# Fourier layer and soft mixture of experts on one core: slot logits of two steps made in one block on TensorE, with the order of the batch chains and the split of copies set anew

## The chip, the core and the metric

The kernel runs on 1 core of one Trainium2 chip, as one launch. The metric is the time of one execution in microseconds (us) as the device gives it; less is better. The program works in fp32; many matmuls are made as three fp32r products of a rounded high part and the rest ("h" and "l" in the names), which gives them nearly fp32's precision.

## What is computed

```python
X = np.fft.rfft(x, axis=1)                      # x: 8 x 2496 x 256
Yr = Xr @ w_r - Xi @ w_i + b_r                  # w: 256 x 256
Yi = Xr @ w_i + Xi @ w_r + b_i
Yr = np.sign(Yr) * np.maximum(np.abs(Yr) - 0.01, 0.0)    # Yi the same
y = np.fft.irfft(Yr + 1j * Yi, n=2496, axis=1)
x = y.reshape(19968, 256)
logits = x @ phi                                # 32 slots, 4 for each of 8 experts
d = np.exp(logits - logits.max(0)); d /= d.sum(0) + 1e-9     # over all tokens
slot_input = d.T @ x
slot_out = np.maximum(slot_input @ w1[e], 0) @ w2[e]         # per expert, F = 1024
c = np.exp(logits - logits.max(1)); c /= c.sum(1) + 1e-9     # over the slots
out = c @ slot_out
```

## The kernel before

**The idea.** 2496 = 39 x 64, so each transform is made in two stages of matmuls, a 39-point one and a 64-point one. The kernel never makes y: phi, the slot sums and the inverse transform are linear, so the slot logits are taken in the frequency domain and transformed back with 32 columns in place of 256, and the slot inputs are summed there as well.

**The work of a batch** (8 batches b) is cut into 5 steps of 4 frequencies (`KG`), so there are 40 steps s, with grp = s mod 5. On TensorE (PE) a step makes:

- `pa` (`a_unit`, L368): the 39-point stage of a later batch, 11 units of three 512-column matmuls for each batch. Its input x is split into `xh` (a rounding copy, line with `E_("ah")`) and `xl` (a subtraction). ScalarE (ACT) copies `pa` to `ast`, which goes through DRAM to `ap`.
- `px` (`f2`, L437): the 64-point stage, two halves; ACT and VectorE (DVE) make `xth`, `xtl`, `xsm`, `xsh` and GpSimd (POOL) `xsl` from it.
- `pk` (`lin_k`, L509) and `py` (`lin_y`, L520): the complex 256 x 256 product, in three real products. DVE adds them to `ut`; the soft threshold is ut - clip(ut): a clip (`TENSOR_SCALAR rt<-ut`, by the table "th") and a subtraction on POOL (`TENSOR_TENSOR rt<-ut,rt`, "tl").
- `pq` (`tp_p`, L550): the slot logits of the step, phi (128 x 32 a half) against `rt`. Only 32 of the array's 128 columns are needed, so four matmuls, one for each frequency, stand side by side in four column strips: L569-576. ACT copies the 128 x 128 result to `lg`, PE transposes it into the same bank, DVE multiplies it with a sign into `p_sb`.
- `pt` (`tp_t`, L586): eight transposes of `rt`; the copies `T` out of PSUM go by the table "te".

**The chain of a batch** (`c_stages`, L671) begins when its `p_sb` is complete and runs beside the steps of the next batches: `pg`, a trip through DRAM, `pL` (logits in the time domain), the maximum over tokens (`pm`, `pb`), exp, the way back (`pe`, DRAM, `pd`) to `dd`, and then the slot sums `pr` (`slots_acc`, L810; five groups of 8 matmuls, 32 columns wide, four side by side like `pq`), which multiply `dd` with the `T` tiles of the batch. `c_comb` (L604) makes the softmax over the slots beside it. For batch 7, `last_chain` (L1064) does the same without DRAM; behind it stand the experts' two layers (`hps`, `po`) and the output loop (`pq<-rhs,ct`), whose 156 matmuls feed the stores of the result.

**What sets the order.** Every piece of work is a generator that yields a due time and then issues its instructions; a heap (`step_to`, `run_until`, L854) runs the earliest first, and one unit of this time is a quarter of a step. Each engine then works strictly in that written order. The due times are the numbers in `PLAN` (L138): "tp" are those of `tp_p`, "tt" those of `tp_t`, "pr", "pm", "pb", "pe", "pd" those of a chain, "late" the ones for batches 4 to 6, "T_" those of the end. A letter string such as "AV" deals the instructions of a kind out in turn: A is ACT, V is DVE, P is POOL. The last 24 clips and subtractions have a table of their own ("lth", "ltl"). All DMA issues on SP keep the written order too. Tiles of one tag share buffers in rotation: `pt`, `pf`, `pl` have two PSUM banks each, `ps` and `pr` one; "T" has 20 tiles, "rt" 4.

Of the kernel before, what the change touches and what calls it, by code (L numbers as in the profile page):

```python
# [220 lines left out]
def fourier_soft_moe_kernel(ctx: ExitStack, tc: tile.TileContext, t: dict, out: bass.AP):  # L221
# [60 lines left out]
    def mm(**kw):  # L282
        tc.keep_in_program_order(nc.tensor.matmul(**kw))  # L283
# [299 lines left out]
    def tr(out, in_, identity):
        tc.keep_in_program_order(nc.tensor.transpose(out=out, in_=in_, identity=identity))  # L584
# [797 lines left out]
```

## Time and profile before

| | us |
|---|---|
| three timed runs | 532.81, 536.44, 533.71 (median 533.71) |
| the profiled execution | 534.27, with a span of 532.4 from the first instruction to the last |
| start, up to the first steps | 0 to 45 |
| the steps of batches 0 to 7 beside the chains | 45 to 427 |
| end of the last steps and the chain of batch 7 | 427 to 456.6 |
| the experts (`hps`, `po`) | 456.6 to 474 |
| output loop and last stores | 474 to 532.4 |

In the profile, a row of the timeline gives the start of an instruction in us from the span's start, its duration, the engine and what it writes and reads; "x16" are 16 neighbouring instructions of one kind. PE is TensorE's matmul, PEld its weight load. An fp32 matmul stands as two instructions. A matmul's duration is longer than the distance to the next start, since matmuls overlap: of dense rows the distance from start to start is the cost. "Idle before" is the time in which the engine did nothing ahead of the instruction, with who released it.

### The profile page before, as it was taken

The numbers are of one execution on the slowest core, as the hardware profiler recorded it, in microseconds if no ns is written. First come the engines' busy times: TensorE is split into PE (matmuls) and PEld (weight loads), VectorE is DVE, ScalarE is ACT, GpSimd is POOL, SyncE is SP. The second block draws the span as 40 slices with busy tenths as digits, with TensorE's granted clock in tenths as the row PEclk, the third lists the DMA queues.
The fourth block names the chain that finished last, engine by engine and source line by source line (L and its number), as shares of the span: only waits on it lengthen the run. The fifth ranks groups of instructions, "written<-read, shape, count | busy, mean of one in ns | idle before, by whom it ended". The sixth has DMA issues, their size and how long they took to land.

```text
span 532.4 us, 12136 instructions
## 1 busy us (share of the span) xinstructions
PE 509.8 (96%) x4512; PEld 437.7 (82%) x4512; DVE 406.1 (76%) x801; ACT 304.5 (57%) x683; POOL 316.8 (59%) x300
## 2 busy tenths in 40 slices
PE   8889999999999999999999999999999999899991
PEld 4478999998999899998989899988989877368880
DVE  3277988689978988998789878987878686337671
ACT  4346565667665766566657656765564336037770
POOL 0049687667976787578757876897457521414210
PEclk9999999999999999999999999999999999899997
DMA  8999575757686667566766666796967489329998
GB/s 299 270 321 321 162 219 159 216 175 151 221 228 175 143 216 211 186 150 217 202 189 147 225 169 204 162 324 170 267 153 187 124 335 372 116 107 388 403 405 326
DMA packets 84799, 119.99 MB, mean 225 GB/s; under 512 B 38380, under 2 KB 59372, under 8 KB 84740
## 3 DMA queue, kind: packets, MB, share of 16 engines
q1 hardware_dynamic: 83796, 117.08, 71.7%
q10 hardware_dynamic: 944, 2.13, 1.4%
q8 instruction: 36, 0.59, 0.5%
q14 instruction: 23, 0.19, 0.1%
HBM read 69.19 MB, written 50.00 MB: 224 GB/s over the span
## 4 chain that ended last, share of the span: by engine, by line
PE 86%; DMA 4%; DVE 4%; ACT 2%; SPq 1%; issue 1%; POOL 0%; DVEq 0%; ACTq 0%
PE py L283 20%; PE px L283 12%; PE pa L283 11%; PE pq L283 10%; PE pk L283 10%; PE pt L584 6%; PE pr L283 3%; PE hps L283 2%; PE pL L283 2%; PE pc L584 2%; PE pd L283 2%; PE pe L283 2%; PE pg L283 1%; PE po L283 1%; DMA ap<-ad 1%; DMA xr<-in_x 1%
## 5 line engine op out<-in xcount | busy, mean ns | idle before, releaser
L217 POOL TENSOR_TENSOR rt<-ut,rt 128x512 f32<-128x512 f32 x79 | 112.6, 1425 | 16.4 <-DVE rt L217 15.8
L217 POOL TENSOR_TENSOR xl<-xr,xh 117x512 fp32r<-117x512 f32 x73 | 99.2, 1360 | 16.5 <-PE py L283 8.8
L217 POOL TENSOR_TENSOR xsl<-xsm,xsh 128x256 fp32r<-128x256 f32 x77 | 59.3, 770 | 77.4 <-DVE xsh L217 54.1
L283 PE MATMUL px<-smov,ap 128*128 128x128 f32 x640 | 85.1, 276 | 1.9 <-ACT ast L217 1.0
L283 PEld LDWEIGHTS px<-smov,ap 128*128 128x128 f32 x640 | 79.9, 191 | 7.4 <-ACT ast L217 2.0
L217 ACT COPY ast<-pa 128x512 f32<-128x512 f32 x85 | 50.0, 589 | 57.2 <-PE pa L283 55.4
L217 DVE SCALAR_TENSOR_TENSOR ut<-py,pk,k 128x256 f32<-128x256 f32 x160 | 69.6, 476 | 13.0 <-PE py L283 11.5
L217 ACT CAST xth<-px 128x512 fp32r<-128x512 f32 x80 | 46.8, 587 | 47.2 <-PE py L283 30.9
L217 DVE TENSOR_TENSOR xtl<-px,xth 128x512 fp32r<-128x512 f32 x80 | 54.6, 684 | 20.0 <-ACT xsm L217 19.6
L217 DVE TENSOR_SCALAR rt<-ut 128x512 f32<-128x512 f32 x69 | 57.3, 831 | 0.5
L283 PE MATMUL py<-xth,nwsh 128*128 128x256 f32 x160 | 54.1, 338 | 0.1
L217 ACT COPY T<-pt 128x512 f32<-128x512 f32 x80 | 47.3, 602 | 1.8 <-PE pt L584 1.8
L283 PE MATMUL pk<-xsh,w_rh 128*128 128x256 f32 x160 | 48.0, 300 | 0.0
L584 PE MATMUL pt<-pk,rt 128*128 128x128 f32 x320 | 47.4, 274 | 0.6 <-DVE p_sb L217 0.3
L283 PE MATMUL pk<-xsl,w_rh 128*128 128x256 f32 x160 | 45.2, 283 | 0.0
L283 PE MATMUL py<-xth,wdh 128*128 128x256 f32 x160 | 45.2, 282 | 0.0
L283 PE MATMUL pk<-xsh,w_rl 128*128 128x256 f32 x160 | 45.1, 282 | 0.0
L283 PE MATMUL py<-xth,wdl 128*128 128x256 f32 x160 | 45.1, 282 | 0.0
L283 PE MATMUL py<-xtl,nwsh 128*128 128x256 f32 x160 | 45.1, 282 | 0.0
L283 PE MATMUL py<-xth,nwsl 128*128 128x256 f32 x160 | 45.1, 282 | 0.0
L283 PE MATMUL py<-xtl,wdh 128*128 128x256 f32 x160 | 45.1, 282 | 0.0
L283 PE MATMUL pq<-rhs,ct 128*128 128x512 f32 x156 | 41.9, 406 | 0.2 <-DVE rhs L217 0.2
(206 smaller groups left out, 1265.7 us busy)
## 6 DMA issues: line engine op xcount, KB each, us to landing
ap<-adr SPq DMA_DIRECT2D x76, 256.0 KB
out<-ost SPq DMA_DIRECT2D x37, 512.0 KB
xr<-in_x SPq DMA_DIRECT2D x35, 512.0 KB
adr<-ast SPq DMA_DIRECT2D x20, 768.0 KB
w<-in_moe_w SPq DMA_DIRECT2D x20, 512.0 KB
w<-in_moe_w SPq DMA_DIRECT2D x18, 256.0 KB
adr<-ast SPq DMA_DIRECT2D x8, 512.0 KB
x<-in_x SPq DMA_DIRECT2D x11, 256.0 KB
```

The lines of the kernel that those rows point to most:

```text
L217: return lambda *a, **k: self.tc.keep_in_program_order(f(*a, **k))
L283: tc.keep_in_program_order(nc.tensor.matmul(**kw))
L584: tc.keep_in_program_order(nc.tensor.transpose(out=out, in_=in_, identity=identity))
```

## The change

**Two steps in one block.** `tp_p` leaves out the odd group of a pair (groups 1 and 3, in all batches but the last); at the next step a new `tp_pair` makes the logits of both steps in one run of matmuls into one PSUM bank (256 columns), with one copy to `lg` (256 wide), two transposes and one multiplication by the sign (256 wide). Group 0 stays alone. `rt` gets a fifth buffer.

**Slot sums with them.** The due times "pr" put the groups of slot sums two by two beside such a block: groups 0 and 1 ahead of the logits of group 0, groups 2 and 3 behind the pair of groups 1+2, group 4 ahead of the pair 3+4.

**Order and split.** `pm`, `pb`, the second `pe` and the second `pd` of a chain come at other due times; `pt` of the first half stands earlier. All `xh` copies of batches 2 to 7 go to ACT ("AV" to "A"), every third clip up to step 27 to POOL ("V" to "VVP"), every fourth `T` copy to DVE ("A" to "AAAV").

**The end.** The last three steps of batch 6's softmax over slots (`cs6`, its reciprocal and the multiplication) come behind the last slot sum; the four zeroed tiles `z1` to `z4` are made together with `z0`, and so take their "T" buffers ahead of the last four weight loads; two dummy matmuls stand on PE between the last slot sum and the next layer.

```diff
-    "ah": 'AV',
+    "ah": 'A',
-    "th": 'V',
+    "th": 'VVP',
-    "pm": 8.5,
-    "pb": 9.8,
-    "pe": [11.35, 12.35],
+    "pm": 9.045,
+    "pb": 10.163,
+    "pe": [11.35, 12.044],
-    "pd": [17.12, 17.75],
-    "pr": [20.49, 24.49, 28.49, 32.489999999999995, 36.489999999999995],
+    "pd": [17.12, 18.008],
+    "pr": [20.48, 20.459, 28.647, 28.49, 36.49],
...
-    "late": {'6': {'cms': [13.1, 13.2, 18, 21.85, 21.9, 22.5],
+    "late": {'6': {'cms': [13.1, 13.2, 18, 22.65, 22.66, 22.67],
-    "T_": {'du': [], 'z': 1.72,
+    "T_": {'du': [[2.55, 2]], 'z': 1.686,
-    "te": 'A',
-    "tp": [0.5, 1.0, 1.9, 1.8],
-    "tt": [2, 2.505],
+    "te": 'AAAV',
+    "tp": [0.5, 1.0, 1.784, 1.8],
+    "tt": [1.616, 2.505],
+    "tpp": [0.5, 0.731, 1.719, 1.8],
...
@@ tp_p
-        yield n + d[0]
+        pair = b < B - 1 and grp > 0
+        if pair and grp % 2:
+            return
+        yield n + (PLAN["tpp"] if pair else d)[0]
...
+        if pair:
+            yield from tp_pair(s, n, PLAN["tpp"])
+            return
...
+    def tp_pair(s, n, d):
+        b, grp = steps[s]
+        pq = psum("pt", f"pq{b}_{grp}")
+        for i in range(2):
+            rv = [tts[(s - 1 + i, e)].rearrange("p j c q -> p j (c q)") for e in range(2)]
+            for e in range(2):
+                for j in range(KG):
+                    mm(out=pq[S * j : S * j + S, 128 * i : 128 * i + 128], lhsT=phr[:, e, :],
+                       rhs=rv[e][:, j], start=(e == 0), stop=(e == 1), skip_group_check=True)
+        yield n + d[1]
+        lg = wtile([128, 256], F32, "lg", f"lg{b}_{grp}")
+        A.copy(out=lg, in_=pq[:, 0:256])
+        yield n + d[2]
+        for i in range(2):
+            tr(pq[:, 256 + 128 * i : 384 + 128 * i], lg[:, 128 * i : 128 * i + 128], ident)
+        yield n + d[3]
+        ks = slice(grp * KG - KG, grp * KG + KG)
+        V.tensor_tensor(out=psb[b][:, ks, :], in0=pq[:, 256:512].rearrange("p (j s) -> p j s", s=S),
+                        in1=sgn[:, ks].unsqueeze(2).broadcast_to([128, 2 * KG, S]), op=ALU.mult)
```

How the order moves on PE, in the steps 17 and 18 (`py3_2`, `py3_3`: batch 3, groups 2 and 3), where the logits of groups 1 and 2 of batch 3 and the slot sums of batch 1 are made. Before, PE has two runs of the 32-column kind there; the first is:

```order
L283 MATMUL pr1_2867<-T1_1_0_1481,dd1_2581 32x256 x2
L283 MATMUL pr1_2867<-T1_1_1_1507,dd1_2581 32x256 x2
L283 MATMUL pq3_1_3053<-rt3_1_0_2849,pk0_112 32x128 x4
L283 MATMUL pq3_1_3053<-rt3_1_1_2921,pk0_112 32x128 x4
L283 MATMUL py3_2_1_3042<-xth3_2_1_2888,nwsh_228 128x256
```

and the second, a step later:

```order
L283 MATMUL pr1_2867<-T1_2_0_1640,dd1_2581 32x256 x2
L283 MATMUL pr1_2867<-T1_2_1_1670,dd1_2581 32x256 x2
L283 MATMUL pq3_2_3216<-rt3_2_0_3031,pk0_112 32x128 x4
L283 MATMUL pq3_2_3216<-rt3_2_1_3087,pk0_112 32x128 x4
L706 MATMUL pm2_3225<-pk0_112,mx2_3197 128x117
```

Now there is one run, at the second place, with both steps' logits and two groups of slot sums; at the first place `py` goes through without a break, and `pm2` is no longer behind the run:

```order
L284 MATMUL pq3_2_3175<-rt3_1_0_2825,pk0_112 32x128 x4
L284 MATMUL pq3_2_3175<-rt3_1_1_2901,pk0_112 32x128 x4
L284 MATMUL pq3_2_3175<-rt3_2_0_3011,pk0_112 32x128 x4
L284 MATMUL pq3_2_3175<-rt3_2_1_3052,pk0_112 32x128 x4
L284 MATMUL pr1_2840<-T1_2_0_1596,dd1_2539 32x256 x2
L284 MATMUL pr1_2840<-T1_2_1_1658,dd1_2539 32x256 x2
L284 MATMUL pr1_2840<-T1_3_0_1750,dd1_2539 32x256 x2
L284 MATMUL pr1_2840<-T1_3_1_1802,dd1_2539 32x256 x2
L284 MATMUL py3_3_1_3168<-xth3_3_1_3029,nwsh_228 128x256
```

Over the whole order of PE, the runs in which only `pq`, `pr` and `pz` (a one-column sum that opens a chain's slot sums) of 32 columns stand fall from 42 to 28: 14 fewer, two in each of the batches 0 to 6.

The end on DVE, from the last two multiplications into `dd` of batch 7 to the copy into `z0`. Before, the sums `cs` of batch 6 stand between them and `zacc`:

```order
L217 TENSOR_TENSOR dd7_6814<-pd7_1_6851,pk1_113 128x320 [waits PE_49]
L217 TENSOR_REDUCE cs6_6585<-cb6_6583 128x22
L217 TENSOR_SCALAR cs6_6585<-cs6_6585 128x22 [waits DVE_49]
L217 RECIPROCAL cs6_6585<-cs6_6585 128x22 [waits DVE_49]
L217 SCALAR_TENSOR_TENSOR zacc_121<-zacc_121,fo_120,pz7_6885 128x1 [waits PE_49,Activation_49]
L217 TENSOR_SCALAR zacc_121<-zacc_121 128x1 [waits DVE_49]
L217 RECIPROCAL zacc_121<-zacc_121 128x1 [waits DVE_49]
L217 TENSOR_SCALAR dgs_123<-pk1_113,zacc_121 128x32 [waits DVE_49]
L217 SCALAR_TENSOR_TENSOR acc_122<-acc_122,fo_120,pr7_6872 128x256 [waits PE_49]
L217 COPY z0_6855<-psl1_6906 128x8x4 [waits PE_49,Pool_49]
```

Now they stand behind that copy, and with them POOL's multiplication `cb6`, which waits for them:

```order
L218 TENSOR_TENSOR dd7_6758<-pd7_1_6795,pk1_113 128x320 [waits PE_49]
L218 SCALAR_TENSOR_TENSOR zacc_121<-zacc_121,fo_120,pz7_6833 128x1 [waits PE_49,Activation_49]
L218 TENSOR_SCALAR zacc_121<-zacc_121 128x1 [waits DVE_49]
L218 RECIPROCAL zacc_121<-zacc_121 128x1 [waits DVE_49]
L218 TENSOR_SCALAR dgs_123<-pk1_113,zacc_121 128x32 [waits DVE_49]
L218 SCALAR_TENSOR_TENSOR acc_122<-acc_122,fo_120,pr7_6820 128x256 [waits PE_49]
L218 COPY z0_6798<-psl1_6857 128x8x4 [waits PE_49,Pool_49]
L218 TENSOR_REDUCE cs6_6529<-cb6_6527 128x22
L218 TENSOR_SCALAR cs6_6529<-cs6_6529 128x22 [waits DVE_49]
L218 RECIPROCAL cs6_6529<-cs6_6529 128x22 [waits DVE_49]
```

What moved is only the place of the three `cs6` instructions; `acc` and the copy into `z0`, on which the experts' first matmul waits, come three instructions earlier.

More of the change, by code (lines that the diff above doesn't have):

```diff
@@ L145 @@
     "c0": 0.05,
-    "pg": [1.35, 2.3],
+    "pg": [1.408, 2.3],
     "pL": [6.6, 7.3],
-    "pm": 8.5,
-    "pb": 9.8,
-    "pe": [11.35, 12.35],
+    "pm": 9.045,
+    "pb": 10.163,
+    "pe": [11.35, 12.044],
     "cm": 14.3,
-    "pd": [17.12, 17.75],
-    "pr": [20.49, 24.49, 28.49, 32.489999999999995, 36.489999999999995],
+    "pd": [17.12, 18.008],
+    "pr": [20.48, 20.459, 28.647, 28.49, 36.49],
     "au": [1.4, 18.85, 19.7],
@@ L158 @@
     "xlo": 1.1,
-    "sho": 0.2,
+    "sho": 0.359,
     "slo": 0.1,
@@ new lines @@
+    "late": {'6': {'cms': [13.1, 13.2, 18, 22.65, 22.66, 22.67], 'pd': [16.681, 16.6], 'pdt': ('pl', 'pl'), 'pr': [17.15, 18.3, 20.179, 19.707, 19.902], 'pL': [6.6, 7.3], 'pm': 8.51, 'pb': 9.45, 'pe': [11.747, 11.6, 12.419], 'pg': [0.875, 1.275], 'fr': {'sinv': 0, 'm2': 0, 'f1': 0, 'suni': 0}, 'pbx': 1.5, 'pet': ('pf', 'pf'), 'so': 0.2}, '5': {'pr': [33.585, 35.378, 40.05, 40.06, 40.157]}, '4': {}},
+    "T_": {'wl': [[-45, 'r', 1], [-44, 'r', 1], [-43, 'r', 1], [-31.0, 't', 1], [-30.7, 't', 1], [-29.4, 't', 2], [-27.8, 't', 2], [-27.6, 't', 2], [-24, 't', 2], [-22, 't', 2], [-20, 't', 2], [-12.5, 'R', 1], [-12.4, 'R', 1], [-11.4, 's', 1], [-11, 'a', 1], [-10.3, 'a', 1], [-9.6, 'a', 1], [-9.5, 'Ww_r', 1], [-8.7, 'Wnws', 1], [-8.6, 'Wwd', 1], [0.01, 'k', 1], [0.01, 'u', 1], [0.02, 'x', 2], [0.02, 'x', 2], [0.02, 'x', 2], [1.4, 't', 2], [1.4, 't', 2], [1.4, 't', 2], [1.4, 't', 2], [1.4, 't', 2], [1.73, 'T', 2], [1.74, 'T', 2]], 'cl': 2.0, 'cp': 46.5, 'ct': 46.6, 'du': [[2.55, 2]], 'd1': [], 'cm': [19.9, 19.91, 19.92, 25, 25.1, 25.2], 'cm7': [0.71, 1.7, 1.95, 2.7, 2.71, 2.8], 'ye': 0.2, 'te': [[5.6, 0.2], [5.5, 0.4]], 'pg': [-17, -13.5, -8.3, -3.934, -2.9], 'yt': 0.578, 'wr': -30.6, 'tp': [0, 0.6, 0.85, 0.5], 'tt': [0.4, 0.55, 0.821, 1.25, 0.994], 'z': 1.686, 'th': [0.1, 0.12], 'tl': [0.2, 0.25], 'pgt': ['ps', 'ps', 'ps', 'pf', 'pf'], 'ch': [0.263, 0.5, 0.7, 1.0, 1.514, 2.0], 'te7': 'AAAAAAAAAA', 'op': 2, 'ot': [3, 5, 7], 'gt': [-16.99, -13.49, -8.290000000000001, -3.9400000000000004, -2.89]},
@@ L197 @@
     "xl0": 1.0,
-    "pbx": 0.45,
+    "pbx": 0.543,
     "pet": ('ps', 'ps'),
@@ L234, in fourier_soft_moe_kernel @@
     a_bufs = {"xr": 3, "xh": 3, "xl": 3, "ast": 3}
-    main_bufs = {"xsm": 2, "k1": 2, "ut": 2, "rt": 4, "lg": 2}
+    main_bufs = {"xsm": 2, "k1": 2, "ut": 2, "rt": 5, "lg": 2}
     chain_bufs = {"wr": NWR, "ap": 3, "xth": 3, "xtl": 3, "xsh": 3, "xsl": 3, "T": 20, "p_sb": 2, "g_sb": 1,
@@ L570, in tp_p @@
         yield n + d[1]
-        lg = wtile([128, 128], F32, "lg", f"lg{b}_{grp}")
-        A.copy(out=lg, in_=pq[:, 0:128])
+        lg = wtile([128, 256], F32, "lg", f"lg{b}_{grp}")
+        A.copy(out=lg[:, 0:128], in_=pq[:, 0:128])
         yield n + d[2]
-        tr(pq[:, 128:256], lg, ident)
+        tr(pq[:, 128:256], lg[:, 0:128], ident)
         yield n + d[3]
@@ L579, in tp_p @@
             in1=sgn[:, ks].unsqueeze(2).broadcast_to([128, KG, S]),
+            op=ALU.mult,
+        )
+    def tp_pair(s, n, d):
[5 more added lines that the diff above has]
+                for j in range(KG):
+                    mm(
+                        out=pq[S * j : S * j + S, 128 * i : 128 * i + 128],
+                        lhsT=phr[:, e, :],
+                        rhs=rv[e][:, j],
+                        start=(e == 0),
+                        stop=(e == 1),
+                        skip_group_check=True,
+                    )
+        yield n + d[1]
+        lg = wtile([128, 256], F32, "lg", f"lg{b}_{grp}")
+        A.copy(out=lg, in_=pq[:, 0:256])
[4 more added lines that the diff above has]
+        ks = slice(grp * KG - KG, grp * KG + KG)
+        V.tensor_tensor(
+            out=psb[b][:, ks, :],
+            in0=pq[:, 256:512].rearrange("p (j s) -> p j s", s=S),
+            in1=sgn[:, ks].unsqueeze(2).broadcast_to([128, 2 * KG, S]),
             op=ALU.mult,
@@ L1020, in slot_stationary @@
     def slot_stationary():
-        pools["slz"] = wtile([128, 2, E, 32], F32, "T", "z0")
-        P.memset(pools["slz"], 0.0)
+        zs = [wtile([128, 2, E, 32], F32, "T", f"z{i}") for i in range(5)]
+        for z in zs:
+            P.memset(z, 0.0)
+        pools["slz"], pools["hz"] = zs[0], zs[1:]
     def ap_load(s):
@@ L1059, in dummy @@
     def dummy(n):
-        dps = psum("ps", f"dps{next(seq)}")
+        dps = psum("pt", f"dps{next(seq)}")
         for _ in range(n):
@@ L1200, in fourier_soft_moe_kernel @@
     P.tensor_copy(out=dmr, in_=dmask)
-    pools["hz"] = [wtile([128, 2, E, 32], F32, "T", f"z{i}") for i in range(1, 5)]
-    for z in pools["hz"]:
-        P.memset(z, 0.0)
     rhs = []
```

2 lines of the change are left out of this document (removed).

## The prediction, made before the changed kernel was run

> **What bounds the kernel now.** I read the page first: which engine is busy, and through which engine the chain runs that ended last. Then one long window over the steps, 45 to 425 us (busy us and count of PE, PEld, DVE, ACT, POOL).
>
> ```profile
> PE 509.8 (96%) x4512; PEld 437.7 (82%) x4512; DVE 406.1 (76%) x801; ACT 304.5 (57%) x683; POOL 316.8 (59%) x300
> PE 86%; DMA 4%; DVE 4%; ACT 2%; SPq 1%; issue 1%; POOL 0%; DVEq 0%; ACTq 0%
> 45.00:425.00 380.00, 377.81 (x3461) 344.66 (x3462) 324.53 (x636) 231.20 (x521) 279.46 (x254) 1.00 0.70 194
> ```
>
> Over the steps PE is busy for 377.81 of 380.00 us at a granted clock of 1.00, DVE for 85%, POOL for 74%, ACT for 61%. PE sets the pace there, so only what shortens PE's own sequence shortens the steps. But a busy PE isn't a dense PE: a matmul's duration covers its successor's start. So I looked in the timeline at distances from start to start, around one run of slot logits:
>
> ```profile
> 63.31 0.28 PE L283 MATMUL py<-xth,wdl 128*128 128x256 f32 x1
> 63.43 0.28 PE L283 MATMUL py<-xtl,wdh 128*128 128x256 f32 x1
> 63.64 0.64 PE L283 MATMUL pq<-rt,pk 128*32 128x128 f32 x16
> 64.22 0.39 PE L283 MATMUL py<-xth,nwsh 128*128 128x256 f32 x1
> 64.44 0.28 PE L283 MATMUL py<-xth,nwsl 128*128 128x256 f32 x1
> ```
>
> Dense `py` rows stand 0.12 us apart (63.31, 63.43). Around the run there is 0.21 from the last `py` to the first `pq`, and 0.22 from the first `py` behind it to the second. The weight load of that first `py` is not hidden either: see the waits below. A later run, with slot sums in front:
>
> ```profile
> 239.20 0.28 PE L283 MATMUL py<-xtl,wdh 128*128 128x256 f32 x1
> 239.41 0.64 PE L283 MATMUL pr<-T,dd 128*32 128x256 f32 x8
> 239.86 0.62 PE L283 MATMUL pq<-rt,pk 128*32 128x128 f32 x16
> 240.41 0.38 PE L283 MATMUL py<-xth,nwsh 128*128 128x256 f32 x1
> 240.64 0.28 PE L283 MATMUL py<-xth,nwsl 128*128 128x256 f32 x1
> ```
>
> It shows the same 0.21 on entry and 0.23 behind, and nothing between `pr` and `pq`: the break belongs to the change between 128 and 32 columns, not to `pq`.
>
> **Term 1, the runs.** What does a run cost beside its work? From the last full matmul ahead to the second behind, the first run takes 64.44 - 63.43 = 1.01, the second 240.64 - 239.20 = 1.44. The second has 8 `pr` more: two rounds of 256 columns, four side by side, cost 0.43. The four rounds of 128 columns of `pq` are as many columns, so 0.43 too. Then 1.01 - 0.43 - 2 x 0.12 = 0.34 is neither kind's work. Taken by `pq`'s own rounds ((0.64 - 0.28) / 3 = 0.12 each, 0.48) it is 0.29. I take 0.33. The order has 42 runs before and 28 after, with the same matmuls in them: 14 x 0.33 = **-4.6** (bounds 14 x 0.29 = -4.1 and 14 x 0.34 = -4.8). This counts in full as long as PE stays the pacemaker.
>
> **Term 2, the waits in the steps.** PE and weight-load rows of the waits (total us, times, longest):
>
> ```profile
> PEld py L283 <- issue: 5.6, 28, 0.2
> PE px L283 <- ACT ast L217: 1.0, 1, 1.0
> PE pa L283 <- POOL xl L217: 0.8, 2, 0.5
> PE pd L283 <- ACT dd L217: 0.5, 1, 0.5
> PEld pd L283 <- ACT dd L217: 2.1, 6, 0.8
> ```
>
> The first row is the exposed load behind the runs again, 0.2 each time, and no gain of its own. The last two go together: the second `pd` of a chain needs the `ps` bank that ACT empties, and came 0.63 units behind the first; now it comes 0.89 behind, with `pt`, two transposes and a `px` between them in the order. I take the matmul's own **-0.5** (bounds 0 and the 2.1 of its loads). The second `pe` comes nearer to the first (0.69 units, 1.0 before), with a `pa` and a `px` still between; I leave that in the next sum. The pair's own waits are covered: its transposes come a full `pt` behind the ACT copy, and it writes only a bank that the earlier logits shared in the same way. The odd group is later by a step, which its chain doesn't feel: a chain begins with group 4, which is not delayed. The fifth `rt` buffer covers the longer hold.
>
> **Term 3, the other engines' load.** Rows by form:
>
> ```profile
> L217 DVE TENSOR_SCALAR rt<-ut 128x512 f32<-128x512 f32 x69 | 57.3, 831 | 0.5
> L217 POOL TENSOR_SCALAR rt<-ut 128x512 f32<-128x512 f32 x11 | 7.0, 639 | 1.6 <-DVE ut L217 1.1 <-PE py L283 0.3
> L217 DVE CAST xh<-xr 117x512 fp32r<-117x512 f32 x34 | 24.9, 731 | 2.2 <-DMA xr<-in_x 2.2
> L217 ACT CAST xh<-xr 117x512 fp32r<-117x512 f32 x39 | 24.5, 632 | 2.1 <-DMA xr<-in_x 2.1
> L217 ACT COPY T<-pt 128x512 f32<-128x512 f32 x80 | 47.3, 602 | 1.8 <-PE pt L584 1.8
> L217 DVE COPY ast<-pa 128x512 f32<-128x512 f32 x3 | 2.1, 688 | 4.8 <-PE pa L283 4.8
> ```
>
> 33 `xh` casts go from DVE to ACT (-33 x 0.731 = -24.1, +33 x 0.632 = +20.9), 18 clips from DVE to POOL (-15.0, +11.5), 17 `T` copies from ACT to DVE (-10.2; +11.7 with the row of a DVE copy of that size out of PSUM). The 14 copies and 14 multiplications saved by the pairs (28 narrow ones become 14 wide ones) are off the path and left out. Sums: DVE -27.4, ACT +10.7, POOL +11.5, that is 78%, 64% and 77% of the window. None reaches PE. Busy shares hide order, though: the clip on POOL stands in the queue ahead of `xl` and `xsl`, for which `pa` and `pk` wait, and ACT's `xh` ahead of the copies that free `px` and `pa` banks. The trace doesn't have these queues. Bounds: 0, and the rows for POOL and ACT above doubled and doubled again (1.0 + 0.8, to four times as much: +5.4). I take **+0.5**, near the low end, because PE shows just three such waits in 380 us. On SP the x loads lose a wait for DVE and keep their place.
>
> **Term 4, the end of batch 7.**
>
> ```profile
> 452.55 0.87 DVE L217 TENSOR_REDUCE cs<-cb 128x22 f32<-128x704 f32 x1
> 453.53 1.05 PE L283 MATMUL pr<-T,dd 128*32 128x256 f32 x16
> 453.88 0.19 DVE L217 SCALAR_TENSOR_TENSOR zacc<-zacc,fo,pz 128x1 f32<-128x1 f32 x1
> 454.04 1.37 POOL L217 TENSOR_TENSOR cb<-cb,cs 128x704 f32<-128x704 f32 x1 [3.72 <-DVE cs L217]
> 454.49 0.96 DVE L217 TENSOR_SCALAR dgs<-pk,zacc 128x32 f32<-128x32 f32 x1
> 455.37 0.47 DVE L217 SCALAR_TENSOR_TENSOR acc<-acc,fo,pr 128x256 f32<-128x256 f32 x1
> 455.89 0.63 PE L283 MATMUL psl<-dgs,acc 128*128 128x32 f32 x4 [1.31 <-DVE acc L217]
> 456.63 3.68 PE L283 MATMUL hps<-w,z 128*32 128x512 f32 x19
> ```
>
> `pr` ends at 454.58, but `acc` starts at 455.37, behind `dgs`. That 128x32 instruction takes 0.96 and ends with POOL's `cb` (454.04 + 1.37 = 455.41); the like-sized small ones beside it take 0.2. With `cs` and `cb` moved behind, `dgs` should end near 454.7, `acc` run from there and `psl` start near 455.2: **-0.7** (bounds 0, and PE's whole idle time, -1.3). The dummies need 4 x 0.11 behind a 32-column run and end by then.
>
> The moved memsets stand on POOL before `cb`, and the last weight loads get "T" buffers freed by later transposes:
>
> ```profile
> 434.01 13.98 SPq L277 DMA_DIRECT2D w<-in_moe_w  x19
> 449.31 1.53 PE L584 MATMUL pt<-pk,rt 128*128 128x128 f32 x12
> 467.80 6.25 PE L283 MATMUL po<-w,z 128*32 128x256 f32 x112
> ```
>
> Their issue moves from 448 to about 451, with `cin0` behind them on SP; the matmuls that read them are the last of `po`, some 20 us later. Nothing; without that cover it would be 3.
>
> **Term 5, the clock.** Four windows of 3.4 us (same columns, then the granted clock):
>
> ```profile
> 454.08:457.50 3.42, 2.00 (x24) 0.83 (x19) 2.53 (x6) 0.18 (x1) 1.33 (x1) 1.00 0.24 91
> 457.50:460.91 3.41, 3.41 (x20) 0.87 (x16) 0.59 (x3) 0.00 (x0) 2.61 (x5) 0.50 0.02 5
> 13.76:17.18 3.42, 2.40 (x6) 0.87 (x6) 0.69 (x1) 0.75 (x2) 0.00 (x0) 1.00 1.02 393
> 24.00:27.42 3.42, 2.05 (x16) 1.86 (x16) 0.83 (x3) 2.14 (x6) 1.27 (x1) 1.00 1.13 241
> ```
>
> Behind the thin stretch at 454 to 457 the clock was 0.50 for 3.41 us, in the middle of `hps`: half of 3.41, 1.7 us lost. Stretches with 2.05 and 2.40 us of matmuls kept 1.00. The change closes 0.7 of the gap and lays dummies into it, so that stretch would hold about 3.0. If the clock then stays, -1.7; but I don't know in how many of the three timed runs it fell (they spread over 3.6 us). Half of it: **-0.85** (bounds 0 and -1.7).
>
> [...]
>
> **The sum.** -4.6 - 0.5 + 0.5 - 0.7 - 0.85 = -6.15 against the profiled execution's 534.27, of which 532.4 is span: 528.1. That execution lies 0.56 above the median of the runs shown, 533.71, and they are what a new measurement repeats: 533.71 - 6.15, rounded, **527.5**. The start (DMA) and the output loop have no edit in them.
>
> **Rivals.**
> 1. *The queues take part of it back* (term 3 near its bound). For it: POOL and ACT at 77% and 64% with strict order, DVE's long softmax pieces between the `T` copies. Against it: three waits in the rows. 527.5 - 0.5 + 5.4 = 532.4, so between 529.5 and 532.5. Chance 0.20.
> 2. *The runs' ends are not saved*: the break stays because a merged run waits for the later `rt`, or `py` at the old place waits for something that the break hid. For it: the odd logits now need two steps' clips. Against it: 0.34 in both runs though one has twice the work. Only terms 4 and 5 remain: 533.71 - 1.55 = 532.2. Chance 0.08.
> 3. *Slower, by ACT's queue.* Place: between `px` and its copies, where a cast of 0.632 now stands in every unit in place of every second one. If PE waits through more than 6.15 / 20.9 = 30% of the moved casts' time, the change loses; at 50% it is +10.4 - 6.15, 538.0. Against it: ACT is idle for 39% of the window. Chance 0.05.
> 4. *The memsets hold up DVE.* Five of them (2.4 us together, as long as z's five before) now lie near 445 to 448, beside DVE's maximum and exp of batch 7. In the trace POOL's `cb` stretched `dgs` by 0.75. If they stretch that chain for their whole time, 527.5 + 2.4 = 529.9. Chance 0.07.
>
> [...]
>
> **How the numbers follow.** The forecast has 0.60, its own range 525.5 to 529.5. Term 1 at -4.8, term 2 at -2.1, term 4 at -1.3 and term 5 at -1.7 together would give 524; they hardly all come. The range reaches up into rivals 1 and 4: 525.0 to 531.0. A measurement tells about 1% of this kernel from no change: 528.4 is that line. Four fifths of the forecast lie below it (0.48), and a little of rival 4 (0.02): faster 0.50; same 0.45, with rivals 1 and 2, the rest of 4 and the forecast's upper end; slower 0.05, rival 3.
>
> **What would show it.** Right: 28 such runs with 0.34 each; about -5 us between 45 and 427; `dgs` at 0.2 and `psl` 0.7 nearer to the last `pr`; the clock at 1.00 through `hps`. Wrong: new PE rows in the waits for `xl`, `ast`, `ea` or `lg` that sum to over 2 us, or a middle stretch as long as before.

## The result, and the profile after

| | before | after |
|---|---|---|
| median of 22 runs each, us | 533.44 (531.66 to 536.44) | 537.51 (534.52 to 541.62) |
| ratio to before, 95% interval | 1 | 1.0076 (1.0058 to 1.0093) |
| the profiled execution, us | 534.27, span 532.4 | 537.36, span 535.6 |

(In brackets behind a median stand the lowest and the highest run. A ratio is taken over all runs of both kernels and needn't be the quotient of the two medians; in the experiments below the two differ by up to 0.25%.)

Instead of some 6 us less, the change costs 4. The page's lines on the busy engines and the chain, and the window over the steps in the same columns as before:

```profile
PE 508.8 (95%) x4516; PEld 439.5 (82%) x4516; DVE 385.8 (72%) x753; ACT 312.8 (58%) x685; POOL 322.3 (60%) x318
PE 76%; DMA 8%; DVE 6%; ACT 3%; issue 2%; SPq 1%; POOL 0%; ACTq 0%; DVEq 0%
45.00:425.00 380.00, 372.78 (x3414) 341.71 (x3412) 300.97 (x583) 236.98 (x515) 281.24 (x268) 1.00 0.69 192
```

PE is busy for 372.8 of the 380 us, where it was 377.8, and holds 76% of the chain, where it held 86%. The load moved the way it was counted, though less of it (DVE down by 23.6 us, ACT up by 5.8, POOL by 1.8, although POOL's clips grew by 10.8 as counted: its other rows fell); no engine is full, and PE has holes. The last `pk`, at 427.1 before, starts at 432.7: the whole loss arises in the steps. PE's waits (total us, times, longest; rows that bear on nothing here are left out):

```profile
PE px L284 <- ACT ast L218: 2.6, 12, 0.3
PE pa L284 <- DMA xr<-in_x: 2.2, 1, 2.2
PE px L284 <- DVE xsm L218: 1.5, 4, 0.4
...
PE pL L284 <- ACT chpL L218: 1.3, 2, 1.1
...
PE pb L284 <- DVE dg L218: 0.7, 2, 0.5
PE pL L284 <- DVE clpL L218: 0.6, 1, 0.6
```

A single wait of 1 us for `ast` has become 12 small ones, and `pL` and `pb` wait for the chain. To see all of it, also the waits that are spread over loads, I summed the distances from one PE row's start to the next less the dense distance of its form (0.12 for 256 columns, 0.23 for 512, 0.11 for 128, and so on), from step 4's first `pk` to step 39's, by the row that came late (us, one profiled execution each; the columns on the right are experiments told below):

| late row | before | after | pairs only | letters only | chain only | xth four | cover | pL later |
|---|---|---|---|---|---|---|---|---|
| ends of the 32-column runs | 18.6 | 13.4 | 16.5 | 18.4 | 18.1 | 13.4 | 13.4 | 12.8 |
| `px` | 1.6 | 8.3 | 6.8 | 1.0 | 1.6 | 5.4 | 3.2 | 6.4 |
| `pL` | 1.8 | 4.4 | 2.9 | 2.1 | 2.2 | 4.4 | 2.4 | 1.6 |
| `pb` and `pe` | 0.7 | 2.4 | 0.3 | 0.7 | 5.7 | 3.6 | 3.6 | 3.2 |
| `pa` | 0.5 | 1.3 | 0.4 | 0.8 | 1.5 | 1.2 | 1.2 | 1.3 |
| `pt` and `pd` | 2.8 | 0.7 | 1.5 | 4.2 | 1.2 | 0.9 | 0.6 | 0.7 |
| rest | -7.8 | -6.6 | -7.5 | -7.7 | -7.7 | -6.8 | -6.9 | -6.3 |
| sum | 18.2 | 23.7 | 20.9 | 19.5 | 22.6 | 22.0 | 17.6 | 19.7 |

(The rest is below nothing because many rows stand a little denser than the figure taken for their form. In the column "cover" the 6.1 us of useless matmuls told below count as work, so its sum is without them.) The runs gave back 5.2 us, a little more than the 4.6 forecast. `px` alone took 6.7, the rows of the chain (`pL`, `pb`, `pe`) another 4.3.

**The place of a `px` wait.** Timeline of the kernel after, PE, ACT and DVE, in a step without logits (start, duration, engine; in brackets how long the engine stood idle and who ended it):

```profile
207.98 1.05 PE L284 MATMUL px<-smov,ap 128*128 128x128 f32 x8
...
209.35 0.28 PE L284 MATMUL py<-xth,wdl 128*128 128x256 f32 x1
...
209.67 0.59 ACT L218 CAST xth<-px 128x512 fp32r<-128x512 f32 x1 [0.90 <-PE py L284]
...
210.15 0.38 ACT L218 COPY xsm<-px 128x256 f32<-128x256 f32 x1
...
210.56 0.69 DVE L218 TENSOR_TENSOR xtl<-px,xth 128x512 fp32r<-128x512 f32 x1 [1.55 <-ACT xsm L218]
...
211.01 0.60 PE L621 MATMUL pt<-pk,rt 128*128 128x128 f32 x4
211.17 0.41 DVE L218 TENSOR_TENSOR xsm<-px,xsm 128x256 f32<-128x256 f32 x1
211.21 0.59 ACT L218 COPY ast<-pa 128x512 f32<-128x512 f32 x1 [0.16 <-PE pa L284]
...
211.76 0.97 PEld L284 LDWEIGHTS px<-smov,ap 128*128 128x128 f32 x8 [0.40 <-issue]
211.80 1.13 PE L284 MATMUL px<-smov,ap 128*128 128x128 f32 x8 [0.19 <-ACT ast L218]
```

`px` is done at 209.0, but ACT starts `xth` only at 209.67: there are three `xth` buffers, and the third was let go by the `py` at 209.35, the last that reads it. From there a chain frees `px`'s bank: `xth`, `xsm`, `xtl`, `xsm`, until 211.58. PE meanwhile has the last six `py`, a `pa` and four `pt`, done at about 211.45, and the next `px` could start there; it starts at 211.80. The page names ACT's `ast`, the other semaphore of that wait. But `ast` empties the other bank. `px`'s first weight load starts at 211.76, while `ast` still runs (to 211.80), and at this place of the kernel before `px` itself starts (210.77) while `ast` runs (210.43 to 211.02). The bank `px` needs is let go by DVE's `xsm`, 0.22 ahead of its start. The kernel before at the same place:

```profile
207.38 0.28 PE L283 MATMUL py<-xth,wdl 128*128 128x256 f32 x1
...
207.75 0.58 ACT L217 CAST xth<-px 128x512 fp32r<-128x512 f32 x1 [0.96 <-PE py L283]
...
208.16 0.62 PE L283 MATMUL pq<-rt,pk 128*32 128x128 f32 x16
...
209.25 0.41 DVE L217 TENSOR_TENSOR xsm<-px,xsm 128x256 f32<-128x256 f32 x1
...
210.77 1.06 PE L283 MATMUL px<-smov,ap 128*128 128x128 f32 x8
```

The same ACT wait (0.96), but a run of slot sums and logits stands between the `py` that lets `xth` go and the next `px`. The bank is free at 209.66, 1.1 us before `px` wants it.

### The profile page after: what moved, and what is told of

The parts are those of the page before. It is cut to its first block, busy times and chain, and to the rows that moved or that the text cites. A ratio compares the mean times of both kernels' runs of the same rounds, so it can differ in the third digit from the quotient of the medians.

```text
span 535.6 us, 12084 instructions
## 1 busy us (share of the span) xinstructions
PE 508.8 (95%) x4516; PEld 439.5 (82%) x4516; DVE 385.8 (72%) x753; ACT 312.8 (58%) x685; POOL 322.3 (60%) x318
## 4 chain that ended last, share of the span: by engine, by line
PE 76%; DMA 8%; DVE 6%; ACT 3%; issue 2%; SPq 1%; POOL 0%; ACTq 0%; DVEq 0%
PE py L284 18%; PE px L284 11%; PE pq L284 10%; PE pa L284 8%; PE pk L284 8%; PE pt L621 5%; PE pr L284 3%; DMA xr<-in_x 3%; DMA gd<-g_sb 2%; DMA gp<-gd 2%; PE pL L284 2%; PE pc L621 2%; PE pe L284 2%; PE pg L284 1%; DVE cb L218 1%
## 5 line engine op out<-in xcount | busy, mean ns | idle before, releaser
L218 POOL TENSOR_TENSOR rt<-ut,rt 128x512 f32<-128x512 f32 x79 | 109.6, 1388 | 21.3 <-DVE rt L218 15.5
L218 POOL TENSOR_TENSOR xl<-xr,xh 117x512 fp32r<-117x512 f32 x73 | 98.0, 1343 | 14.7 <-DVE xh L218 8.3
L284 PE MATMUL py<-xth,nwsh 128*128 128x256 f32 x160 | 52.4, 327 | 0.1
L218 ACT CAST xh<-xr 117x512 fp32r<-117x512 f32 x72 | 45.4, 633 | 2.0 <-DMA xr<-in_x 1.9
L621 PEld LDWEIGHTS pt<-pk,rt 128*128 128x128 f32 x320 | 38.0, 141 | 3.7 <-issue 0.2
```

The lines of the kernel that those rows point to most:

```text
L218: return lambda *a, **k: self.tc.keep_in_program_order(f(*a, **k))
```

## The experiments

Each time is compared with runs of the kernel before on the same chip (medians 533.66 to 534.72), in five rounds. The theories in the expectations: **Q**, ACT's and DVE's queues with the moved casts and copies (the split letters) make `px` and `pa` late. **C**, the new due times of the chain do. **F**, the loop from `px` over its copies to the next `px` is a floor that the saved runs only uncover. **W**, F made precise: the chain of 2.1 us above against PE's work in the short step. **L**, in the denser program what one place no longer waits for is waited for at the next.

**The four parts apart.** The changed kernel without one part, and the kernel before with one part. (Where values stand side by side in a diff below, they are cut out of longer lines of the kernel.) First the letters taken back:

```diff
-    "ah": 'A',  "th": 'VVP',  "te": 'AAAV',
+    "ah": 'AV', "th": 'V',    "te": 'A',
```

> The changed kernel with the three split letters put back as before (xh casts alternately on ACT and DVE, all clips on DVE, all T copies on ACT); pairs, chain order and tail stay changed. Theory Q (the engines' queues: the moved casts and copies make ACT and DVE free px's and pa's banks late): most of the some 10 us of new PE waits go, 537.5 - 5 to 8 = 529.5 to 532.5, and the waits of px for ast fall from 12 to a few. Theory C (the chain order: the second pe nearer to the first, pm, pb, pd later): little changes, 536 to 538. Theory F (the loop px, its copies, px is a floor that the saved runs only uncover): under 1.5 us of change, 536 to 538.

Measured: 539.49, ratio 1.0088 (1.0056 to 1.0121). Not faster. Q, as the cause of the loss, falls.

The chain's due times taken back:

```diff
-    "pg": [1.408, 2.3], "pm": 9.045, "pb": 10.163, "pe": [11.35, 12.044], "pd": [17.12, 18.008], "pbx": 0.543
+    "pg": [1.35, 2.3],  "pm": 8.5,   "pb": 9.8,    "pe": [11.35, 12.35],  "pd": [17.12, 17.75],  "pbx": 0.45
```

> The changed kernel with the chain's due times (pg, pm, pb, pe, pd, pbx) put back as before; pairs, split letters and tail stay changed. Theory C: the new waits go, 530 to 533. Theory Q: 536 to 538, since ACT's and DVE's queues are as long as in the changed kernel. Theory F: 536 to 538.

Measured: 536.45, 1.0028 (0.9996 to 1.0059). The time itself lies where Q and F had it; by the ratio, some 60% of the loss goes, though `pm` now cuts five merged runs in two (33 runs). The interval just touches the changed kernel's (1.0058 to 1.0093), so this run alone doesn't settle C.

The tail alone:

```diff
-'cms': [13.1, 13.2, 18, 21.85, 21.9, 22.5]   'du': []          'z': 1.72
+'cms': [13.1, 13.2, 18, 22.65, 22.66, 22.67] 'du': [[2.55, 2]] 'z': 1.686   (with slot_stationary and dummy)
```

> The kernel before with the edits of batch 7's end alone (combine work of batch 6 behind the last sum, five memsets on POOL early, dummies on PE). By the traces of the two kernels the tail gave 0.67 from the end of the steps to hps and up to 1.7 in hps where the clock did not halve. All theories: 533.4 - 0.7 to 2.4 = 531.0 to 532.7; if the clock's dip only moves with time and does not come from the thin stretch, 532.7.

Measured: 533.4, 0.9973 (0.9948 to 0.9998), that is -1.4 by the ratio (-0.1 to -2.8), within the gain of 0.7 to 2.4 that was expected; the medians are 0.8 apart.

The pairs alone (`tp_pair`, `tpp`, `pr`, five `rt`):

> The kernel before with the pairs of logits alone (14 fewer 32-column runs, slot sums due with them, the fifth rt buffer); split letters, chain order and tail as before. Theories Q and C: the pairs' saving comes through, 533.4 - 4 to 5 = 528.5 to 529.5. Theory F: what the runs save comes back as waits for px's banks, 532.5 to 534.

Measured: 536.71, 1.0049 (1.0018 to 1.0081). Slower by 2.6, although PE has nine runs fewer (in this order, too, `pm` cuts five). In the table `px` waits 5.2 more with letters and chain as they were. That is F's direction, and worse than F said.

The other way round, the changed kernel with the pairs alone undone:

> The changed kernel with the pairs alone undone (every group's logits in a run of their own, 42 runs again, four rt buffers, slot sums due as before); split letters, chain order and tail stay changed. Theory W (the pairs' short steps lose it): no more waits behind pt, and what stays is the tail's gain: 531.5 to 533.5, faster than the changed kernel although PE pays 14 runs more. Theories Q and C (letters or chain lose by themselves): 535 to 538, or 537.5 + 4.6 if the pairs' saving counts in full.

Measured: 537.84, 1.0080 (1.0056 to 1.0104). With the rest of the change in place, 14 runs more or fewer make no difference that can be seen; and the rest loses by itself. W said faster and fails on that point. Two parts of the rest are run apart next. Three more due times of the change are in none of the four parts, and no run has them alone: `tp` (1.9 to 1.784), `tt` (2 to 1.616, the earlier `pt`) and `sho` (0.2 to 0.359, the time of DVE's `xsh`). The letters alone:

> The kernel before with the three split letters of the change alone (all xh casts on ACT, every third clip on POOL, every fourth T copy on DVE). Theory Q (rival 3 of the prediction): +3 to +5, 536.5 to 538.5, by ACT's and DVE's queues ahead of px's copies. Theory C (the chain order loses): 533 to 534.5.

Measured: 535.99, 1.0020 (0.9995 to 1.0045): between the two expectations, at most a small loss. The chain's due times alone:

> The kernel before with the chain's due times of the change alone (second pe ahead of six py, second pd behind px, pm behind the run and pb behind px). Theory C: +3 to +5, 536.5 to 538.5, by waits of pe, pb and px, since ACT stands at the second pe ahead of xth. Theory Q: 533 to 534.5.

Measured: 537.5, 1.0071 (1.0043 to 1.0099): +3.8 us, the largest of the four. C holds here, but by `pb` and `pe` (table: 0.7 to 5.7), not by `px`. This place in its timeline shows why `pb` is late:

```profile
221.30 0.26 PE L706 MATMUL pm<-pk,mx 117*128 117x117 f32 x1
...
221.89 0.74 POOL L217 TENSOR_TENSOR xsl<-xsm,xsh 128x256 fp32r<-128x256 f32 x1 [2.54 <-DVE xsh L217]
221.94 0.70 DVE L217 TENSOR_TENSOR mall<-mall 128x1 f32<-128x1 f32 x1
...
222.59 1.27 POOL L217 TENSOR_TENSOR rt<-ut,rt 128x512 f32<-128x512 f32 x1
...
222.68 1.22 DVE L217 TENSOR_SCALAR dg<-pk,mall 128x32 f32<-128x32 f32 x1
...
223.95 0.39 PE L283 MATMUL pb<-dg,ones 128*117 128x32 f32 x2 [0.23 <-DVE dg L217]
```

and before:

```profile
219.33 0.32 PE L706 MATMUL pm<-pk,mx 117*128 117x117 f32 x1
...
220.00 0.16 DVE L217 TENSOR_TENSOR mall<-mall 128x1 f32<-128x1 f32 x1
220.19 0.24 DVE L217 TENSOR_SCALAR dg<-pk,mall 128x32 f32<-128x32 f32 x1
...
220.91 0.30 PE L283 MATMUL pb<-dg,ones 128*117 128x32 f32 x2
```

In the old place `pm`'s followers on DVE met an idle POOL. Put behind the run they meet POOL's `xsl` and `rt`: the 128x1 `mall` takes 0.70 and ends with `xsl` (222.64 and 222.63), the 128x32 `dg` takes 1.22 and ends with `rt` (223.90 and 223.86). It is so in most batches; the rows by form, first before, then with the chain alone (min/median/max ns):

```profile
L217 DVE TENSOR_SCALAR dg<-pk,mall x7: 241/241/242, 113.8 to 426.5; 128x32 f32<-128x32 f32 x7
```

```profile
L217 DVE TENSOR_SCALAR dg<-pk,mall x7: 242/1211/1216, 114.4 to 430.4; 128x32 f32<-128x32 f32 x7
```

From `pm` to `pb` it is now 2.65 where it was 1.58, and the chain's next steps (`exp`, `chpe`, `clpe`) can start only behind it. `pe` waits as well (three times for `clpe`, 1.5 us); how much of that comes from the stretched `dg` and how much from the second `pe`'s nearer due time, no run tells apart.

**The hole behind `pt`.** A fourth buffer for `xth`, so that ACT need not wait for `py`:

```diff
-"xth": 3,   f1a = wmp.tile([PX, QA], F32, tag="f1a", name="f1a")
+"xth": 4,   f1a = wtile([PX, QA], F32, "g7", "f1a")
```

> The changed kernel with a fourth buffer for xth (f1a moves into another tile's place to make room; no engine's order changes). Theory W: in the steps that now have no logits, px waits for a chain that begins when py lets an xth buffer go (xth 0.59, xsm 0.38, xtl 0.69, xsm 0.41: 2.1 us), while PE has only six py, a pa and four pt (1.9 us) to do; the run stood in that stretch and covered it. With a fourth buffer xth begins some 0.55 earlier, and the 12 waits of 0.38 behind pt go: -4 to -5, 532.5 to 533.5. Rival L (DVE and ACT as a whole are too loaded in the short steps, their queues set it): the start of xth isn't what matters, 536.5 to 538.

Measured: 535.77, 1.0033 (1.0012 to 1.0055), so -2.3 against the change's 1.0076, half of what W expected. The mechanism is as W has it, at the same place:

```profile
208.06 1.05 PE L284 MATMUL px<-smov,ap 128*128 128x128 f32 x8
...
209.16 0.59 ACT L218 CAST xth<-px 128x512 fp32r<-128x512 f32 x1 [0.30 <-PE px L284]
...
211.09 0.60 PE L621 MATMUL pt<-pk,rt 128*128 128x128 f32 x4
...
211.53 1.06 PE L284 MATMUL px<-smov,ap 128*128 128x128 f32 x8
```

`xth` follows its own `px`, and the next `px` stands 0.44 behind `pt`, with no gap. But `pb` and `pe` wait 1.2 more in the table: a part is taken back, which is the direction of L.

The control, the kernel before with a fourth buffer:

> Control: the kernel before with the fourth xth buffer. Theory W: a run stands in every one of those stretches there, and no wait behind pt over 0.13 is seen: no change, 532.5 to 534.5. If the buffer helps in itself, at any density of PE: -2 or more.

Measured: 534.51, 1.0005 (0.9979 to 1.0030): the buffer does nothing where the run covers the chain.

Useless work laid into the hole (an odd group's four transposes are made twice; 6.1 us more of PE):

```diff
-        for jj in range(2):
+        for jj in (0, 1, 0, 1) if h == 0 and grp in (1, 3) and b < B - 1 else (0, 1):
```

> The changed kernel with useless work on PE: the four transposes of an odd group ahead of px, in just the 14 places where the logits were taken away, are made twice (the second time the same values into the same bank): 14 x 0.44 = 6.1 us more for PE. Theory W: the stretch has a hole of 0.38 there, so about 12 x 0.38 = 4.5 of the 6.1 cost nothing: 538 to 540. If PE is dense there and the waits are made elsewhere: 537.5 + 6.1 = 543.6.

Measured: 537.26, 1.0062 (1.0036 to 1.0087). Six us of matmuls more, and no time more: even W expected some 1.5. PE does not set the pace there. The same place:

```profile
210.38 1.04 PE L621 MATMUL pt<-pk,rt 128*128 128x128 f32 x8
210.54 0.42 DVE L218 TENSOR_TENSOR xsm<-px,xsm 128x256 f32<-128x256 f32 x1
...
211.26 1.06 PE L284 MATMUL px<-smov,ap 128*128 128x128 f32 x8
```

The chain ends at 210.96 and `px` follows eight `pt` at their dense distance (0.88), without a wait.

Shortening the chain instead, by telling `xtl` ahead of ACT's `xsm`:

> The changed kernel with DVE's xtl told ahead of ACT's xsm copy, so that it waits for xth alone; in the traces it starts behind xsm, 0.38 later than xth would let it, and the chain that frees px's bank is as much longer. DVE's order moves too: xtl ahead of a clip. Theory W: the chain of 2.1 us gets 0.3 to 0.4 shorter and the waits of 0.38 behind pt nearly go, 533 to 534.5. Rival L: 536.5 to 538.

Measured: 550.17, 1.0296 (1.0266 to 1.0326). Far slower: DVE now waits twice for each `px`, 53.0 us for `xth` and 17.0 for `xsm`, where the changed kernel waits 44.0 for `xsm`, and the clip and the chain's `clpL` and `clpe` stand behind (`pL` and `pe` are late by 3.5 and 3.8 us more). The order that moved costs more than the chain gained; between W and L this run doesn't tell.

Filling the hole with work that is needed anyway, the odd groups' second four transposes from behind `pk`:

```diff
-PLAN["tt"][h]
+PLAN["tt"][0 if h and grp in (1, 3) else h]
```

> The changed kernel with the odd groups' second four transposes moved from behind pk to ahead of px, the place where the 0.38 was waited, 14 times 0.44 of work that is needed anyway. Theory W: the waits behind pt go and nothing is added: 537.5 - 4 to 5 = 532.5 to 533.5, unless the place behind pk now waits in its stead (the first py of the step comes 0.44 earlier). Rival L (the load of DVE and ACT in the short steps sets the pace, whatever PE's order): 536 to 538.

Measured: 537.06, 1.0067 (1.0040 to 1.0093): no gain, against W. (Its profiled execution was its shortest, 533.93, so its trace can't explain the median.)

**Towards a version that gains.** The fourth buffer and the old chain with `pm` just ahead of the run (8.45); and the moved transposes besides:

> The changed kernel with the fourth xth buffer and the chain's due times as before, but pm just ahead of the merged run, so that it doesn't cut it in two as it did when only the due times were put back (33 runs there, 28 here). If the three effects add (xth -2.0, chain -1.0, five runs less 5 x 0.56 = -2.8): 531.7, so 531 to 533.5. If what one place no longer waits for is waited for at the next (pb, pe, pL, pa: Rival L): 534.5 to 536.

> The kernel of the chain order with the fourth xth buffer, and the odd groups' second transposes ahead of px besides. If the effects add: 529.5 to 532, faster than both kernels. Rival L: 533 to 536.

Measured: 536.59, 1.0055 (1.0033 to 1.0077), and 536.87, 1.0035 (1.0009 to 1.0061). The parts did not add up: at 8.45 `pm` came too early for its input, and lost 3.2 and 4.2 us in the sum of distances, where it had lost nothing.

So `pm` and `pb` left as changed, but `pe`, `pd` and `pg` back, with moved transposes and fourth buffer; and the same with the old letters, where `sho` and `pbx` are back at their old values too:

> The changed kernel with pe, pd and pg due as before (pm and pb stay, so that the runs stay 28), the odd groups' second transposes ahead of px and the fourth xth buffer. Theories W and C: px's and pe's waits both go, 537.5 - 4.5 - 1.5 = 531 to 533. Rival L (what one place no longer waits for is waited for at the next): 534.5 to 537.

> As the one with pe back, but with the split letters of the kernel before too: pairs, tail, pm and pb of the change, the odd groups' second transposes ahead of px, the fourth xth buffer. If the letters lose (Q): 529.5 to 531.5, faster than both kernels. If the letters are needed with the pairs, as the run with letters back alone suggests: 533 to 536.

Measured: 534.24, 1.0009 (0.9988 to 1.0030), and 536.58, 1.0034 (1.0008 to 1.0060). In the first the loss is gone. The second is slower in the middle, but the intervals overlap and two due times differ besides, so whether the new letters are worth keeping isn't shown. What stands in the first one's waits next is `pL` for `clpL` (1.5 us, four times). So `pL` is put later, and in the last kernel `pb` and `pe` too:

```diff
-    "pL": [6.6, 7.3],      "pb": 10.163,  "pe": [11.35, 12.35],
+    "pL": [7.05, 8.02],    "pb": 10.4,    "pe": [11.7, 12.6],     (the last two in the last kernel alone)
```

> The kernel with pe back, the transposes ahead of px and the fourth xth buffer (534.2), with the first pL six py later and the second behind px: between them PE has a pa and a px, 1.6 us, where it waited 0.4 to 0.6 for DVE's clpL. If waits add up (W): -2 to -3, 531 to 532.5. Rival L: 533.5 to 535.5, with pm or pb waiting longer.

> As the one with pL later, with pb behind pk (1.4 us later) and pe half a unit later too. If waits add up (W): another -1.5 to -2.5, 529 to 531, faster than both kernels and than the kernel with the tail alone. Rival L: 533 to 535.5.

Measured: 533.08, **0.9960 (0.9934 to 0.9987)**, and 533.34, 0.9978 (0.9948 to 1.0008). The first beats the kernel before and the changed one; the second is no better than it. PE's waits of the first:

```profile
PE px L284 <- DVE xsm L218: 3.2, 5, 1.1
PE px L284 <- DMA ap<-ad: 1.8, 2, 1.3
PE pa L284 <- DMA xr<-in_x: 1.6, 1, 1.6
...
PE pa L284 <- DVE xsm L218: 1.4, 1, 1.4
PE pe L284 <- DVE clpe L218: 0.7, 1, 0.7
...
```

`pL`'s waits for `chpL` and `clpL` are gone (1.6 in the table, below the 1.8 of before), but `px` waits for DVE's `xsm` again, five times. L is right in this: a kernel with all these repairs is 2.1 us faster than before (0.40%), and the tail alone gives 1.4 of that, so little is left of the 5.2 saved at the runs.

## Why the prediction was wrong, point by point

**The step that failed first** is in term 1: "This counts in full as long as PE stays the pacemaker", with the sentence it stands on, "only what shortens PE's own sequence shortens the steps". The size was right. A merged run in the changed kernel:

```profile
186.62 0.28 PE L284 MATMUL py<-xtl,wdh 128*128 128x256 f32 x1
186.83 0.64 PE L284 MATMUL pr<-T,dd 128*32 128x256 f32 x8
187.29 1.06 PE L284 MATMUL pq<-rt,pk 128*32 128x128 f32 x32
188.27 0.39 PE L284 MATMUL py<-xth,nwsh 128*128 128x256 f32 x1
188.50 0.28 PE L284 MATMUL py<-xth,nwsl 128*128 128x256 f32 x1
```

188.50 - 186.62 = 1.88; less 0.43 for `pr`, twice 0.43 for `pq` and 0.24 for `py`, 0.35 is left. There are 28 such runs, and the table has 5.2 less at their ends. But "PE is busy for 377.81 of 380" says that PE is the last to come everywhere, not by how much the others come before it. At the place shown they had 1.1 us to spare; the change took a run of about as much, and the logits' transposition, out of just that stretch, and made the run of another step longer, where nobody needed the time. So two steps in five became shorter than the chain that frees `px`'s bank. The sign of being wrong that the prediction named, PE rows for `ast` of over 2 us, came (2.6), though what PE waited for there was `xsm`. Rival 2 ("the runs' ends are not saved") asked the near question and looked at the wrong place: the run's own neighbours.

**The second** is in term 2: "The second `pe` comes nearer to the first [...]; I leave that in the next sum". The next sum, term 3, counted only moved casts, clips and copies, and had no chain in it; `pm` and `pb`, moved as well, were in no term. The chain's new times alone cost 3.8 us (2.3 to 5.3). What makes them dear, as far as `dg` shows it, was in my own term 4, where a small DVE instruction, `dgs`, took 0.96 beside POOL's `cb`. I used that for the one `dgs` and did not ask which other small DVE instruction the change puts beside a POOL one: `dg` took 0.24 with POOL idle and 1.21 beside its `rt`.

**Term 2's other half** held: `pd` no longer stands in the waits, and `pd` and `pt` together are late by 2.1 less in the table.

**Term 3**, +0.5 with bounds 0 and +5.4: the letters alone gave +1.1 (-0.3 to +2.4), within the bounds. **Rival 3** named nearly the time that came (538.0), but by luck: its cause isn't this one, for with the casts back the kernel is no faster.

**Term 4**, -0.7, held to the hundredth. The tail of the kernel after:

```profile
459.15 1.05 PE L284 MATMUL pr<-T,dd 128*32 128x256 f32 x16
...
460.12 0.24 DVE L218 TENSOR_SCALAR dgs<-pk,zacc 128x32 f32<-128x32 f32 x1
...
460.27 0.48 DVE L218 SCALAR_TENSOR_TENSOR acc<-acc,fo,pr 128x256 f32<-128x256 f32 x1
460.81 0.63 PE L284 MATMUL psl<-dgs,acc 128*128 128x32 f32 x4
461.58 1.50 PE L284 MATMUL hps<-w,z 128*32 128x512 f32 x12
```

`dgs` takes 0.24, and from this `pr` to `psl` it is 1.66 where it was 2.36. Nothing is seen of **rival 4**: the tail as a whole gave -1.4 with its five memsets in it, and in the kernel after DVE's `fo<-mall` took 0.15 beside them (at 453.02, the memsets to 453.50).

**Term 5**, -0.85: through `hps` the clock was 1.00,

```profile
461.58:464.99 3.41, 3.41 (x32) 1.26 (x36) 1.85 (x5) 0.00 (x0) 1.38 (x1) 1.00 0.03 9
17.96:21.37 3.41, 3.41 (x6) 1.28 (x5) 0.55 (x2) 1.17 (x2) 0.00 (x0) 0.50 0.61 183
```

and a dip of the same length lay at 18 us instead (17.96 to 21.37). Of the five profiled kernels with the old tail two had the dip in `hps` (the kernel before, and the one with a fourth `xth` buffer, where the clock was 0.58 from 457.0 to 460.4), of the fifteen with the new tail none, while dips elsewhere came and went in both. So half of the 1.7 was a fair price, though two in five are few and nothing else shows that a thin stretch brings the dip, and the tail's -1.4 fits the two terms' -1.55 together, with an interval that would fit much else.

**The sum by parts**: tail -0.27%, pairs +0.49%, letters +0.20%, chain +0.71%, together +1.13%; all at once +0.76%. Forecast in the same order were -1.55, -4.6, +0.5 and -0.5 us. The difference isn't clear of the noise: each part's interval is 0.25 to 0.32% wide to either side, which makes some 0.55% for their sum, and the sum lacks `tp`, `tt` and `sho`. The pairs, at +0.49% alone, show no cost where the rest of the change is in place. What stays open: whether the parts overlap at all, what those three due times do, and whether runs of the changed kernel scatter more (7 us among 22, where the kernel before had 5, but also over 7 among 30 in one round of experiments). That the `px` hole takes 6 us of work for nothing is shown; that the moved transposes alone gave nothing for it is measured and not explained.

## What to carry to other kernels

A bound engine at 99% is a statement about who comes last, not about slack: before work is taken out of one step, look up in the timeline by how much each buffer that this step waits for was early, and compare it with what is taken out. Work that is merged into some steps makes the others shorter, and those must be checked, not the mean. When an instruction is moved, ask on each engine of its chain what will run beside it; here a DVE step of 0.24 cost 1.21 in its new place.

## What the runs showed of the hardware

- Two small DVE instructions on SBUF, one of them 128x1, ended with the POOL instruction beside them: `dg` took 241 ns with POOL idle (kernel before), 1211 beside POOL's `rt` (1.27 us; the chain's due times alone), `mall<-mall` 159 with POOL idle, 704 beside `xsl`. They ended 0.01 to 0.05 us behind it. Not every DVE instruction did so: the reduction out of PSUM ahead of them (`mall<-pm`) took 271 to 280 with POOL running or idle, and the 117x96 copy `mx<-mx` in SBUF took 253 with POOL idle and 253 with POOL's `rt` running through it (kernel before, at 425.23).
- A pass between full matmuls and 32-column ones cost the same 0.33 to 0.35 us whether 16 or 48 of them lay in between (1.01 at 63.43 in the kernel before and 2.31 at 165.65 in the kernel after, from the last full matmul ahead to the second behind, less their own work).
- Dips of the clock to 0.50 for 3.41 us (at 457.50 in the kernel before, at 17.96 in the kernel after) came and went with the execution: of the twenty profiled ones two had one in `hps`, eight had one somewhere between 17 and 395 us, and ten had none between the start and the output loop.
